# Five and six kept V tiles instead of six and five, and four gradient tiles instead of five, in a decode layer with its gradients

## The chip, the cores and the metric

The kernel runs on one core of one Trainium2 chip. The core has five engines that run on their own and meet at semaphores: TensorE (PE, matrix products and transposes), VectorE (DVE), ScalarE (ACT), GpSimd (POOL) and SyncE (SP, which here only issues DMAs). PEld is the weight load of PE, which overlaps its products. Sixteen DMA engines move data between the main memory (HBM) and the on-chip memory (SBUF); SP, POOL and ACT each feed them through a queue of their own. The metric is the device time of one execution in microseconds, as a median of several.

## The reference

One decode step (one query token for each of B = 2 batches) of a transformer layer, and the gradients of all its inputs but one. With D = 640, H = 32 heads, a cache of 4096 positions and head width 128:

```
h  = x + softmax(q @ k_cache^T * Dh**-0.5) @ v_cache @ wo     q = layernorm(x) @ wq, per batch and head
h2 = h + relu(layernorm(h) @ w1) @ w2
out, vjp = jax.vjp(f, x, k_cache, v_cache, wq, wo, w1, w2)
return (out, *vjp(grad_out))
```

The large arrays are the two caches, 64 tiles (batch, head) of 1 MB each, and their two gradients, of the same size. For one (batch, head) with probabilities p, output gradient go and scaled query qs, the gradient of V is the outer product of p and go, and that of K the outer product of p * (V @ go - dot) and qs. So V is needed twice: once for the output, and again, when the output's gradient is known, for V @ go. The rest is small: the weights (some 5 MB of wq and of wo, 2 MB of w1 and of w2) are read, and their gradients are rank-2 outer products that are written.

## The kernel before, in words

The order of all instructions is written out by hand: Python generators yield after a few instructions each, and the main loop (L1116) decides which generator goes on. The order on an engine is the order in which the loop calls.

**First pass (`p1_iter`, L449), i = 0 to 65.** At step i it loads and transposes K of pair i on PE and computes its scores, turns the scores of pair i-1 into exponentials and multiplies them into K (`pk`, DVE L464), and for pair i-2 multiplies V with that (`m_ps`, PE L457). An iteration has eight parts, k = 0 to 7. The K tile of pair i-1 is given back in part k=5 (L549), the V tile of pair i-2 in part k=7 (L567).

**Second pass (`p2_iter`, L823), one call per turn j = 0 to 64.** A turn reads a V tile again (W in the code), transposes it on PE (`pair_transpose`, `t_ps`), gets V @ go (`dp_ps`), and writes two tiles of 1 MB: gV of turn j and gK of turn j-1. DVE makes each in two halves (`outer_half`, L818, some 1.2 us a half), and POOL stores it (L875 and L856). `turns` (L396) is the order of the pairs in this pass.

**How the passes overlap.** From i = 41 (P2_AT) on, every second iteration of the first pass carries a turn, so that turns 0 to 11 lie in it, turns 12 and 13 in its last two iterations, and turns 14 to 64 behind it. Around both run generators in the background: `middle_gen` (the MLP forward and backward, then `go_group`, which makes go for groups of heads), `fin_gen` (weight gradients, through `ot` tiles that ACT fills and stores) and `gx_gen` (the gradient of x). `fin_gen` and `gx_gen` start when the second batch's w1 work is over.

**Kept tiles.** `KEPT` says how many V tiles at the end of each batch are not given back after the first pass: they stay in SBUF (L564) and the batch's turns begin with them, so they are not loaded again. With (6, 5), 53 of the 64 V tiles are loaded twice. A kept tile holds its place from its load in the first pass to its turn.

**The tiles.** Twelve places of 1 MB in SBUF serve K, V, W, w2 and at first wq (`ld`). `take` takes the place that has been free longest, `give` returns it, and a tile can change its purpose on the way: `share` sets how many places each of the purposes `ld` (loads), `g` (gradient tiles), `f` (`ot` tiles of `fin_gen`) and `q` (wq, w2 and rows of `gx_gen`) is to own, and a place that is given back goes to a purpose that has too few. In the overlap three of the twelve become `g`. Behind the first pass two places are added, and (L1123 and L1133)

```
share(ld=KEPT[1] + 4, g=5)
...
elif fin is not None and j >= H + KEPT[1] - 1:                # L1133
    share(ld=5 + more, g=5 + 2 * more, f=3, q=2 + 3 * more)
```

divides the fourteen: nine for loads, of which five hold kept tiles, and five for gradients. `f` gets one more place (L1145) when `fin_gen` starts. The second `share` holds from turn 36 on. When go is known for all heads, six more places come (L1127: one `ld`, two `g`, three `q`).

**Loads.** `queue` (L1067) lists them in a fixed order: K of i, V of i-2, and W one turn ahead. `pump` issues the next one as soon as `take` has a place, so a load stands in SP's order behind the program step that gave the place back, and on the chip it waits for the last reader of that place. A tile that DVE writes (gK, gV) waits for the DMA that stored the place before.

`go_group` runs over groups of heads: in batch 0 the kept heads first in two groups, (first, first+2) and (first+2, H), then the others by eight; in batch 1 the kept ones in one group, then the others. `MID` (L404) decides which of the heads of batch 0 keep their 128x128 map (L570) in which of two pools.

Of the kernel before, what the change touches and what calls it, by code (L numbers as in the profile page):

```python
# [15 lines left out]
def kernel(  # L16
# [80 lines left out]
    def goes_to(tag):  # L97

        if owned[tag] > wanted.get(tag, len(pools)):
            for other in homes:  # L100
                if owned[other] < wanted.get(other, 0):
                    return other
        return tag
# [14 lines left out]
    def share(**want):  # L118

        wanted.clear()  # L120
        wanted.update(want)
        for tag in homes:
            while free[tag] > 0 and goes_to(tag) != tag:
                to = goes_to(tag)
                homes[to].append(homes[tag].pop(0))
                for d in (free, owned):
                    d[tag] -= 1
                    d[to] += 1

    def more_home(tag, pool):  # L130
        homes[tag].append(len(pools))
        pools.append(pool)
        free[tag] += 1
        owned[tag] += 1
# [257 lines left out]

    pairs = [(b, h) for b in range(B) for h in range(H)]
    NP1 = len(pairs)
    KEPT = (6, 5)
    turns = [(b, h) for b in range(B) for h in (*range(H - KEPT[b], H), *range(H - KEPT[b]))]  # L396
    turn_of = {bh: j for j, bh in enumerate(turns)}
    kept = {(b, h) for b in range(B) for h in range(H - KEPT[b], H)}
    u_bank = [None]
# [3 lines left out]
    MTs = {}  # L403
    MID = H - KEPT[0] - NMT[1]  # L404
    mt_free = [list(range(n)) for n in NMT]
# [313 lines left out]
    def middle_gen(b):  # L719
# [66 lines left out]

        first = H - KEPT[b]
        bounds = [(first, first + 2), (first + 2, H)] if b == 0 else [(first, H)]
# [6 lines left out]
    def ga_gen():  # L795

        gbc = cols.tile([128, Dff], BF16, tag="fbc", name="gbc")
        for b in range(B):
            yield from bcast_cols(one(gc, b), ND, lambda c: 128, gbc[:, b * D:(b + 1) * D])
        for k in range(NW2):  # L800
            while k not in w2_tiles:
                yield 0.0
            t = w2_tiles.pop(k)
            for c in range(k * FP, min(NF, (k + 1) * FP)):
                kc = f_kc(c)
                for b in range(B):
                    yield from turn()
                    ttr(t[0:kc, c - k * FP, :], gbc[0:kc, b * D:(b + 1) * D], ga[0:kc, b, c:c + 1], D, kc)
                    yield 0.9
            give(t)  # L810
# [122 lines left out]
    def fin_gen(fin):  # L933
        FIN["wide"] = [fin.tile([128, 4, 4, 32], BF16, tag="wide", bufs=2, name="wide") for _ in range(2)]
        for w in FIN["wide"]:
            nc.vector.memset(w[:], 0.0)
        yield from wait(2)
        yield from rows_of(fin, acol, NF, "ar", "rX")
        yield from rows_of(fin, gc, ND, "gr", "rD")
        yield from outer_rows(FIN["ar"], Dff, FIN["gr"], D, out_7, Dff // 96)  # L940
        yield from rows_of(fin, ghfc, NF, "ghfr", "rX")
        yield from rows_of(fin, x2c, ND, "x2r", "rD")
        yield from outer_rows(FIN["x2r"], D, FIN["ghfr"], Dff, out_6, ND)
        HH = H // 2
        while ("gh1", B - 1) not in done:
            yield
        yield from rows_of(fin, gh1c, ND, "gh1r", "rD")
        for s0 in range(0, H, HH):
            yield from rows_of(fin, OFc[:, s0:s0 + HH, :], HH, "OFr", "rX")
            yield from outer_rows(FIN["OFr"], HH * 128, FIN["gh1r"], D, out_5[s0 * 128:(s0 + HH) * 128, :], HH)  # L950
        yield from rows_of(fin, x1c, ND, "x1r", "rD")
        for s0 in range(0, H, HH):
            while not all(("go", B - 1, h) in done for h in range(s0, s0 + HH)):
                yield
            yield from rows_of(fin, GQc[:, s0:s0 + HH, :], HH, "GQr", "rX")
            yield from outer_rows(FIN["x1r"], D, FIN["GQr"], HH * 128, out_4[:, s0 * 128:(s0 + HH) * 128], ND)
# [87 lines left out]
    def bg_until(mark):  # L1044
        slot[0] = 99
        forced[0] = True
        while mark not in done:
            assert bg and bg_one(bg) >= 0.0, mark
        forced[0] = False
# [33 lines left out]
    def pump():  # L1083
        while queue:
            what, k = queue[0]
            if what == "w":
                load_weights(k)
            else:
                tag = "ld"
                if free["ld"] < 1:  # L1090
                    return
                if what == "w2":
                    w2_tiles[k] = load_w2(k, tag)
                else:
                    load_tile(what, k, tag)
            queue.pop(0)
# [12 lines left out]
    def p2_step():  # L1109
        nonlocal g2  # L1110
        try:
            next(g2)
        except StopIteration:
            g2 = None

    for n, (i, j) in enumerate(plan):  # L1116
        all_go = all(("go", B - 1, h) in done for h in range(H))
        if i is None and plan[n - 1][0] is not None:
            pkp.release()
            big1 = tc.alloc_tile_pool(name="big1", bufs=1)  # L1120
            for _ in range(2):
                more_home("ld", big1)
            share(ld=KEPT[1] + 4, g=5)  # L1123
        if all_go and not late[0]:
            wop.release()
            big3 = tc.alloc_tile_pool(name="big3", bufs=1, side="right")
            for tag in ("ld", "g", "g", "q", "q", "q"):  # L1127
                more_home(tag, big3)
        late[0] = all_go
        more = int(late[0])  # L1130
        if fin is not None and not bg2 and not bg3:
            share(ld=8 + 3 * more, g=7 + 3 * more)
        elif fin is not None and j >= H + KEPT[1] - 1:  # L1133
            share(ld=5 + more, g=5 + 2 * more, f=3, q=2 + 3 * more)
        if j is not None:
            while g2 is not None:
                p2_step()
            if j < NP1:
                bg_until(("go", *turns[j]))
            g2 = p2_iter(j, 0)  # L1140
        if i is None and ("w1", 1) in done and fin is None:
            wts.release()
            fin = tc.alloc_tile_pool(name="fin", bufs=1)
            big2 = tc.alloc_tile_pool(name="big2", bufs=1)
            more_home("f", big2)  # L1145
            banks.update(sps=[2, 3], o=[4, 5, 6])
            bg2.append(("fin", fin_gen(fin)))
            bg3.append(("gx", gx_gen(fin)))
        if i == 12:
            bg.append(("ga", ga_gen()))  # L1150
        if i == H + 2:
            banks["bc"].insert(0, banks["sps"].pop(0))
        elif i == P2_AT:
            banks["bc"].remove(7)
            banks["sps"].insert(0, banks["bc"][0])
            banks["bc"] = [7]
        rate = RATES[0 if i is not None and i <= H + 1 else 1 if j is None and i < P2_AT else
                     2 if i is not None else 3 if j <= H else 4]
        if i is None:
            spread[0] = 2  # L1160
            at_k[0] = 1
            k = 0
            while g2 is not None:
                p2_step()
                pump()
                slot[0] = int(k in ((1, 3, 5) if j <= H else (1, 4)))
                k += 1
                bg_step(0, rate)
                bg_step(1, RATE2)
                bg_step(2, RATE3)  # L1170
            continue
        at = MIXED if j is not None else REST
        for k, _ in enumerate(p1_iter(i, i < H + 1, 0)):
            for _ in range(at.get(k, 0)):
                if g2 is not None:
                    p2_step()
            if k == 5:
                a_heads(i)
            pump()

            spread[0] = 1 if i < P2_AT else 2
            at_k[0] = k
            if i >= P2_AT:
                slot[0] = int(k == 6 or (k == 1 and j is None))
            elif i > H + 1:
                slot[0] = {1: 2, 3: 1, 4: 1, 6: 1}.get(k, 0)
            else:
                slot[0] = int(k in (1, 6))
            bg_step(0, rate)
            bg_step(1, 0.0)  # L1190
        if i is not None and i in (H + 1, NP1 + 1):
            bg.append((f"m{i // H - 1}", middle_gen(i // H - 1)))
# [41 lines left out]
```

## Time and profile before

| | |
|---|---|
| median of 3 runs | 908.89 us (908.7 to 909.97) |
| span of the profiled execution, first to last instruction | 905.5 us |
| its mean granted TensorE clock | 0.780 |
| busy PE, PEld | 742.8 us (82%), 620.3 us (68%) |
| busy DVE, ACT, POOL | 696.1 us (77%), 444.7 us (49%), 192.4 us (21%) |
| DMA | 362.87 MB, mean 401 GB/s |
| Vt, Kt loads, issue to landing (median) | 15.9 us, 16.0 us |
| Wt loads | 11.8 us |
| gV, gK stores | 14.7 us, 14.4 us |

No separate time is recorded for the profiled execution; what is known of it is its span, which lies 3.4 us below the median of the timed runs.

How to read it: an engine's share is an average over the whole span. The profile gives busy times and DMA rates for any stretch of it too, and the kernel has several stages: the first pass alone (to about 266 us), the overlap (to about 463 us), and the second pass alone. The DMA row counts how long its sixteen engines had packets, GB/s what they moved: both matter, for a queue with little in it can look busy and move less. Where an engine waits, the profile names the instruction or the DMA that ended the wait.

### The profile page before, as it was taken

The numbers are of one execution on the slowest core, as the hardware profiler recorded it, in microseconds if no ns is written. First come the engines' busy times: TensorE is split into PE (matmuls) and PEld (weight loads), VectorE is DVE, ScalarE is ACT, GpSimd is POOL, SyncE is SP. The second block draws the span as 40 slices with busy tenths as digits, with TensorE's granted clock in tenths as the row PEclk, the third lists the DMA queues.
The fourth block names the chain that finished last, engine by engine and source line by source line (L and its number), as shares of the span: only waits on it lengthen the run. The fifth ranks groups of instructions, "written<-read, shape, count | busy, mean of one in ns | idle before, by whom it ended". The sixth has DMA issues, their size and how long they took to land.

```text
span 905.5 us, 24516 instructions
## 1 busy us (share of the span) xinstructions
PE 742.8 (82%) x10205; PEld 620.3 (68%) x10205; DVE 696.1 (77%) x1286; ACT 444.7 (49%) x1096; POOL 192.4 (21%) x330
## 2 busy tenths in 40 slices
PE   3999899899998997987968854877899879859880
PEld 3887788788887887876857744655667656645560
DVE  2666787777888796777869698986898349989982
ACT  1444343344554564554543434644576656637750
POOL 1344433443211110010011111211122111111120
PEclk9999999999999899999885776655555555555655
DMA  8999999999879999999999999999999999999997
GB/s 361 420 409 403 409 398 410 420 417 388 335 306 377 377 406 425 421 424 421 411 398 392 411 423 394 423 398 396 407 401 388 426 420 423 419 423 416 419 421 296
DMA packets 56254, 362.87 MB, mean 401 GB/s; under 512 B 5680, under 2 KB 11696, under 8 KB 15312
## 3 DMA queue, kind: packets, MB, share of 16 engines
q1 hardware_dynamic: 34704, 212.18, 58.1%
q0 software_dynamic: 18432, 134.23, 35.9%
q10 hardware_dynamic: 3008, 14.91, 4.2%
q8 instruction: 80, 1.31, 0.6%
q14 instruction: 30, 0.25, 0.1%
HBM read 212.16 MB, written 149.13 MB: 399 GB/s over the span
## 4 chain that ended last, share of the span: by engine, by line
PE 42%; DMA 25%; DVE 18%; issue 6%; ACT 6%; SPq 1%; POOL 0%; POOLq 0%; ACTq 0%; DVEq 0%
PE t_ps L423 18%; DMA Vt<-in_A_v_cache_dram 13%; PE m_ps L457 9%; DVE gV L818 5%; DMA out_dram<-gV 4%; DVE gK L818 4%; DMA out_dram<-gK 3%; PE s_ps L436 3%; ACT t_sb L428 3%; DMA wqs<-in_A_wq_dram 3%; DVE gxj L644 2%; PE u_ps L486 2%; PE o_ps L922 2%; PE dp_ps L436 2%; DVE pk L464 2%
## 5 line engine op out<-in xcount | busy, mean ns | idle before, releaser
L428 ACT COPY t_sb<-t_ps 128x512 f32<-128x512 f32 x479 | 274.4, 586 | 214.6 <-PE t_ps L423 208.9
L436 PEld LDWEIGHTS <-t_sb 128*128 128x128 bf16 x4096 | 179.0, 102 | 47.0 <-issue 18.8
L423 PE MATMUL t_ps<-ident_f,Wt 128*128 128x128 f32 x848 | 196.5, 379 | 0.2 <-ACT t_sb L428 0.2
L457 PE MATMUL m_ps<-pk,Vt 128*128 128x129 bf16 x2048 | 171.0, 222 | 19.5 <-DMA Vt<-in_A_v_cache_dram 18.2
L464 DVE TENSOR_TENSOR pk<-Kt,ep 128x2048 bf16<-128x2048 bf16 x128 | 156.5, 1223 | 33.9 <-PE m_ps L457 15.8
L818 DVE TENSOR_TENSOR gK<-rb,gsp 128x2048 bf16<-128x2048 bf16 x128 | 152.4, 1225 | 18.4 <-DMA out_dram<-gV 16.4
L818 DVE TENSOR_TENSOR gV<-rb,pp 128x2048 bf16<-128x2048 bf16 x128 | 153.0, 1219 | 15.1 <-DMA out_dram<-gK 12.5
L423 PE MATMUL t_ps<-ident_f,Kt 128*128 128x128 f32 x1024 | 155.1, 284 | 6.6 <-DMA Kt<-in_A_k_cache_dram 6.3
L423 PEld LDWEIGHTS t_ps<-ident_f,Wt 128*128 128x128 f32 x848 | 135.7, 196 | 35.1 <-issue 29.3
L457 PEld LDWEIGHTS <-Vt 128*128 128x128 bf16 x2048 | 124.5, 98 | 51.0 <-issue 29.7
L423 PEld LDWEIGHTS t_ps<-ident_f,Kt 128*128 128x128 f32 x1024 | 112.6, 144 | 10.9 <-PE s_ps L436 4.6
L474 POOL COPY pk<-ep 128x16 bf16<-128x16 bf16 x80 | 83.2, 1042 | 163.6 <-ACT ep L512 87.8
L436 PE MATMUL dp_ps<-gom,t_sb 128*128 128x2 bf16 x2048 | 95.6, 168 | 8.5 <-ACT t_sb L428 7.5
L875 POOL DMA_DIRECT2D out_dram<-gV x64 | 34.2, 534 | 268.0 <-DVE gV L818 207.7
L856 POOL DMA_DIRECT2D out_dram<-gK x64 | 34.0, 532 | 264.9 <-DVE gK L818 207.8
L436 PE MATMUL s_ps<-qm,t_sb 128*128 128x2 bf16 x2048 | 87.4, 164 | 1.5 <-DVE t_sb L426 1.5
L928 ACT CAST ot<-o_ps 128x512 bf16<-128x512 f32 (+4 forms) x160 | 70.4, 490 | 14.8 <-DMA out_dram<-ot 11.2
L571 ACT CAST MT<-m_ps 128x128 bf16<-128x128 f32 x64 | 17.1, 267 | 104.3 <-PE m_ps L457 104.2
L845 ACT ACTIVATE rb<-dp_ps,rt 128x256 bf16<-128x256 f32 x64 | 30.3, 474 | 69.4 <-PE dp_ps L840 68.7
L644 DVE CUSTOM_DVE_ANT_0 junk<-wo_t,hbc 128x640 bf16<-128x640 bf16 x64 | 52.4, 819 | 0.2
L644 DVE CUSTOM_DVE_ANT_0 gxj<-wqs,gqr 128x1024 bf16<-128x1024 bf16 x40 | 48.8, 1221 | 2.4 <-DMA wqs<-in_A_wq_dram 2.2
L831 DVE SCALAR_TENSOR_TENSOR gsp<-dp_ps,negdot,P_bf 128x64 bf16<-128x64 f32 x64 | 18.0, 281 | 42.3 <-PE dp_ps L436 42.0
(198 smaller groups left out, 719.5 us busy)
## 6 DMA issues: line engine op xcount, KB each, us to landing
Kt<-in_A_k_cache_dram SPq DMA_DIRECT2D x64, 1024.0 KB, 16.0
Vt<-in_A_v_cache_dram SPq DMA_DIRECT2D x64, 1024.0 KB, 15.9
out_dram<-gV POOLq DMA_DIRECT2D x64, 1024.0 KB, 14.7
out_dram<-gK POOLq DMA_DIRECT2D x64, 1024.0 KB, 14.4
Wt<-in_A_v_cache_dram SPq DMA_DIRECT2D x53, 1024.0 KB, 11.8
wq_t<-in_A_wq_dram SPq DMA_DIRECT2D x5, 1024.0 KB, 9.2
wo_t<-in_A_wo_dram SPq DMA_DIRECT2D x4, 1280.0 KB, 19.1
wqs<-in_A_wq_dram SPq DMA_DIRECT2D x5, 1024.0 KB, 17.1
```

The costliest lines, as they stand in the source:

```text
L423: nc.tensor.transpose(t_ps[:, j, :], natf[:, 2 * cc:2 * cc + 2, :].rearrange("p c k -> p (c k)"), ident_f[:])
L428: nc.scalar.copy(out=t_sb[:], in_=t_ps[:])
L436: nc.tensor.matmul(dst[:, sc:sc + 2], lhsT=v[:, j, :, par], rhs=vecs[:, par, :], start=(par == 0), stop=(par == 1))
L457: nc.tensor.matmul(r["m"][:, 0:129], lhsT=r["V"][:, sc, :], rhs=r["pk"][sc // HALF][:, sc % HALF, 0:129], start=(sc == 0), stop=(sc == NSC ...
L464: nc.vector.tensor_tensor(out=p["pk"][k][:, :, 0:128].rearrange("p s (a two) -> p s a two", two=2), in0=p["K"][:, sl, :].rearrange("p s (a ...
L474: nc.gpsimd.tensor_copy(out=col, in_=e)
L644: nc.vector.tensor_tensor_reduce(out=junk[0:kc, 0:width], in0=in0, in1=in1, scale=1.0, scalar=0.0, op0=ALU.mult, op1=ALU.add, accum_out=acc)
L818: nc.vector.tensor_tensor(out=pairs_view(dst[:, sl, :]), in0=row.rearrange("p (a two) -> p a two", two=2)[:, None, :, :].to_broadcast([128 ...
L845: nc.scalar.activation(out=rb[:], in_=bank[:, 128:384], func=ACT.Copy, scale=rt[:, b, h:h + 1])
L856: nc.gpsimd.dma_start(out=natural(out_2, bp, hp), in_=gK[:])
L875: nc.gpsimd.dma_start(out=natural(out_3, b, h), in_=gV[:])
L928: nc.scalar.copy(out=ot[0:P, k, n0:n0 + nn], in_=o_ps[0:P, 0:nn])
```

## The change

```
-    KEPT = (6, 5)
+    KEPT = (5, 6)
...
             big1 = tc.alloc_tile_pool(name="big1", bufs=1)
             for _ in range(2):
                 more_home("ld", big1)
-            share(ld=KEPT[1] + 4, g=5)
+            share(ld=KEPT[1] + 4, g=4)
```

The first batch keeps five V tiles and the second six. `KEPT` is used in four more places: the order of the turns (L396), the set of kept pairs (L398), `MID` (L404), and the bounds of the groups in `middle_gen` (L787). So turn 5 is now a head whose V is loaded again, and turn 37 (head 31 of batch 1) one whose V was kept; the second `share` holds from turn 37 instead of 36. With `KEPT[1]` = 6, the first `share` gives loads ten places, of which six hold kept tiles, and gradients four, so that the sum stays fourteen. The number of tiles loaded twice stays 53.

## The prediction

> **What bounds the kernel now.** I read the page first (span, DMA and its GB/s, HBM bytes), then busy time and DMA rate by stretch, then the chain of waits with PE's and SP's timelines at two places where loads come late, and last what VectorE (DVE) waits for in the stage with the changed `g`.
>
> ```profile
> span 905.5 us, 24516 instructions
> DMA  8999999999879999999999999999999999999997
> GB/s 361 420 409 403 409 398 410 420 417 388 335 306 377 377 406 425 421 424 421 411 398 392 411 423 394 423 398 396 407 401 388 426 420 423 419 423 416 419 421 296
> HBM read 212.16 MB, written 149.13 MB: 399 GB/s over the span
> ```
>
> The transfers set the time. The slices top out near 424 GB/s; 362.87 MB at that rate would take 856 us, so 905.5 holds about 50 us in which DMA was not full. The change moves no byte in total, so its price is only how much of those 50 us it fills or adds. Where are they? By stretch (last two columns: DMA's busy share, GB/s):
>
> ```profile
> 200.00:310.00 110.00, 103.33 (x1758) 90.70 (x1755) 88.24 (x216) 56.89 (x157) 24.16 (x39) 0.97 0.92 357
> 310.00:450.00 140.00, 123.56 (x1987) 108.49 (x1987) 108.33 (x217) 74.36 (x206) 14.17 (x24) 0.94 1.01 418
> 450.00:460.00 10.00, 9.29 (x165) 7.78 (x163) 8.79 (x18) 5.06 (x14) 2.02 (x3) 1.00 0.95 351
> 480.00:530.00 50.00, 43.73 (x586) 39.49 (x586) 41.65 (x76) 25.49 (x47) 9.28 (x21) 0.65 1.00 403
> 560.00:660.00 100.00, 79.66 (x741) 64.41 (x741) 84.38 (x145) 54.81 (x125) 18.37 (x37) 0.57 1.01 404
> 660.00:700.00 40.00, 37.78 (x338) 28.38 (x337) 36.22 (x68) 28.98 (x67) 10.15 (x18) 0.54 0.98 392
> 700.00:890.00 190.00, 150.98 (x1332) 110.55 (x1331) 153.85 (x208) 111.42 (x235) 30.37 (x63) 0.55 1.01 420
> ```
>
> From 200 to 310 PE is busy 94% and DMA moves 357 GB/s: compute sets the pace and loads wait for tiles. From 310 to 450 DMA is full. From 480 to 700 it is nearly full (392 to 404), and from 700 on full again (420).
>
> **Part A, one V tile fewer kept in batch 0.** Following `take` and `give` through the plan, from i=33 to turn 5 (i=51) one more of the 12 tiles carries loads, and every K and V load moves one place ahead. V of i=43, now issued at i=43 k=7, goes out at k=6. That load is the one place before 310 us where PE stands still for data:
>
> ```profile
> 282.08 9.89 DMA Vt<-in_A_v_cache_dram
> 292.02 0.64 PE L457 MATMUL m_ps<-pk,Vt 128*128 128x129 bf16 x8 [2.36 <-DMA Vt<-in_A_v_cache_dram]
> ```
>
> PE waits 2.36 us, and the windows then show its granted clock at 0.57 for 8 us (292 to 300). SP's V loads around it stand at 288.96 and 300.94, 12.0 us apart, where the neighbours are 7.3: 4.7 us lost. With the change K45 goes out at about 273.4 instead of 280.38 and V43 at 280.4, before the queue fills, and the stall should be gone. Behind 310 us transfers set the pace, so what counts is bytes moved earlier. One tile more ahead is 1.049 MB / 424 GB/s = 2.5 us. The dip after the stall, 300 to 307 at 318 GB/s, lost 7 x (1 - 318/424) = 1.75 us, of which I take half, since compute bounds part of it. Sum -3.3 us, bounds -4.7 (the whole late iteration) and 0 (the lead is used up before 310).
>
> The reload that this costs (turn 5's V, 1 MB) enters at i=47 and leaves the last stage: 29 W loads in a row become 28. Both places are full of transfers (418 and 404 to 420), so 2.5 us move and the sum is 0. Its issue on SP takes 0.33 us; SP only waits for tiles there, so nothing stands behind it but later loads that have no tile yet. Group (0..8) of batch 0 is due at turn 5 instead of 6. It is recorded in turn 4's iteration, two iterations ahead of need, so nothing is forced: 0. If that cover were gone, its eight products of 0.82 us (L644) would stand in front of the turn: 6.6 us. Groups of 2+3 instead of 2+4 heads, 6 instead of 5, and the map tiles of L570 are the same work in another place: 0.
>
> **Part B, one V tile more kept in batch 1.** From V of i=58 on one tile fewer carries loads, until turn 37 has used the last kept one. V61 cannot go out with K63:
>
> ```profile
> 425.31 1.57 SPq L444 DMA_DIRECT2D Vt<-in_A_v_cache_dram  x1
> 437.99 0.33 SPq L444 DMA_DIRECT2D Wt<-in_A_v_cache_dram  x1
> 439.18 0.33 SPq L444 DMA_DIRECT2D Vt<-in_A_v_cache_dram  x1
> ```
>
> The first of these rows is V61. It must now wait for K60's tile, which today goes to the W load at 437.99, and each later load slips a place. SP issues nothing between 427 and 438, and the queued megabytes keep DMA at 410 to 426. With one less it runs out 2.5 us earlier, and 450 to 460 (351 GB/s) has no spare work to fill it: +2.5 us. Behind SP's waiting instruction stand the W loads of turns 12 to 14. W of turn 14 would go out at about 462.3 instead of 455.0 and is due at 468.8; V of i=43 above took 9.9 us to land, so PE may stand about 3 us. PE is idle from 470 to 478 anyway, waiting for DVE, which covers it; without that cover 3 us more. Bounds 0 and +5.5.
>
> **Part C, four gradient tiles instead of five, turns 14 to 36 (463 to about 656 us).** What DVE waits for in this stretch, and two stores from the chain with their time to landing:
>
> ```profile
> DVE gK L818 <- DMA out_dram<-gV: 15.0, 8, 4.0
> DVE gV L818 <- DMA out_dram<-gK: 8.5, 7, 2.3
> 584.02 18.62 DMA out_dram<-gK
> 612.40 21.59 DMA out_dram<-gV
> ```
>
> DVE waits 15 times, 23.5 us, for a store to free a tile. With four, a half tile may start when the store four back has landed, not five back. Setting each start between 455 and 645 against the landing of the store four back gives 68 us of overlap in place of 23.5, were landings unchanged. They are not: a full queue lands its stores sooner when fewer stand in it. In 535 to 550 PE does nothing, no loads go out, and stores alone keep DMA at 423 to 429, so there a late DVE costs nothing. What costs is the emptier queue in the dips. The nearest rows: 700 to 890 has six more tiles (one `ld`, two `g`, three `q`) and 420 GB/s, 560 to 660 has 404. That is 2.7 GB/s for a tile, over some 195 us 2.7/404 x 195 = 1.3 us. A tile taken from few is worth more than one added to many, so I take +2.0. Lower bound -1 (fewer stores ahead of each W load). Upper bound: the stretch's loss today, 195 x (1 - 404/424) = 9 us, doubles.
>
> The Trainium skill bears on this part twice. Its page "DMA: Bandwidth & Descriptors", section "Anatomy of one DMA — SWDGE (gpsimd) path", gives a store as about 2.0 us plus bytes over 436 GB/s; an estimate from it is 4.4 us for this megabyte, and by it three stores in flight would suffice and part C would be 0. The trace's first store, alone in its queue, does land in 4.3 us; under load the rows above show 18.6 and 21.6, so I do not use it. Its page "Perfetto Trace Analysis", section "Optimization Strategy", says that the same gap repeating on the engine that should be saturated can mean too few buffers for the next tile; the 15 waits of DVE are such gaps, and by that rule the change goes the wrong way here, by a price it does not state.
>
> **Part D, the output tiles.** `share` at L1134 now waits for turn 37, so `f` gets its second and third tile one turn later. In the built order the 18 `ot` tiles fall behind, and the last is taken at turn 62 instead of 60. Stores of `ot` go out at 664.5, 672.9 and 677.5 now, in a stretch at 392 GB/s; one of them moves out of it into a full stretch. Half a megabyte to one is 1.2 to 2.5 us: I take +1.3, bounds 0 and +5 (two move). At the end two turns of 5.5 us (gV stores at 875.71, 881.47, 886.80) put the last `ot` at about 882, before the last gK store at 889.39, which lands 14.4 later; that covers it.
>
> **Sum.** -3.3 + 2.5 + 2.0 + 1.3 = +2.5 us. On the profiled execution's span: 905.5 to 908.0. The median of the runs, 908.89, lies 3.4 above that span, and I leave this difference as it is: **911.4 us**. The forecast's own range is 910.7 to 914.5.
>
> **The rivals.**
> The lead holds (faster): part A gives its full 4.7, B is hidden because DMA has queued stores at 440 to 460, and C and D are near 0.5 together, as stores alone keep DMA at 425. For it: the stall and the 12.0 us iteration are plain in the trace, and full stretches don't care for one tile. Against: the tile that is given at 33 is taken back at i=58, some 220 us later. 908.9 - 4.7 + 0.5 = 904.7.
> The starved ring (slower, more): DVE, 96% busy from 760 to 860 and 84% from 560 to 660, becomes the bound in turns 14 to 36, because each fifth tile was what let it work ahead while W loads took the queue. Its price is up to part C's 9 us, from the point where DVE's waits pass about 45 us; with B and D and less A: 908.9 + 9 + 3.8 - 3.3 = 918.4. Against: DMA is full there with stores alone.
> A swap (no change): A and B are the same tile at two places and cancel, C and D are hidden by the full queue: 908.9.
>
> **How the numbers follow.** Two runs of this kernel can't be told apart within about 0.2%, 1.8 us. Forecast (+1.8 to +6) 0.40, starved ring (over +6) 0.15, lead holds 0.28, swap 0.17. So faster 0.28, same 0.17, slower 0.55. The range reaches beyond the faster rival's centre to 903.5 and close to the starved ring's, 918, which leaves out about 0.2.
>
> **What would show it.** A: no PE wait of over 2 us on V between 280 and 300, no half clock there, and the gV store of turn 2 (305.35 now) some 4 us earlier. B: a gap in DMA between 425 and 460, V61 issued near 438 less A's gain, 450 to 460 under 351 GB/s. C: DVE waits for stores over 35 us between 455 and 660, with the rate there under 402; if waits grow and the rate stays, C is 0. D: `ot` stores later by one to two turns, and 660 to 700 under 392. I am wrong if the end of the first loop does not move up by about 3 us, or if the last stage, from the first turn without i to the end, does not lengthen.

## The result, and the profile after

The changed kernel takes 913.62 us, the median of 22 runs (908.84 to 919.13); 22 runs of the kernel before beside it have a median of 909.31 us (905.15 to 914.26). The ratio is 1.0042, 95% interval 1.0024 to 1.0060: 3.8 us slower (2.2 to 5.5). A second set of runs gave 1.0042 again (1.0011 to 1.0073). The forecast was 2.5 us slower, 911.4 us, with a range of 903.5 to 918; the result lies in it, on the side that had most of the chance.

Single executions of one kernel differ by about 1% here (35 runs of the kernel before: 904.59 to 915.94), so two profiles differ by some us in places where the programs are the same. Below, a reading counts as shown only where it returns in several kernels with the same part, or in the times; what rests on one profile or one run is called so.

The page of the changed kernel:

```profile
span 909.3 us, 24519 instructions
DMA  8999999999889999999899999999999999999997
GB/s 363 419 410 404 409 399 410 421 417 400 340 306 367 422 423 422 422 421 423 356 387 423 389 424 386 395 394 411 378 399 384 399 371 425 425 424 427 423 424 320
HBM read 212.16 MB, written 149.13 MB: 397 GB/s over the span
```

No byte was added, and the mean rate fell from 399 to 397 GB/s. The dips have moved: 356 and 387 in the 20th and 21st slice (432 to 477 us), 378 and 384 between 636 and 705, 371 at 727 to 750.

Busy time by stretch of the changed kernel, in the columns of before (PE, PEld, DVE, ACT, POOL, granted clock, DMA's busy share, GB/s):

```profile
200.00:310.00 110.00, 105.16 (x1829) 92.57 (x1828) 91.68 (x217) 61.03 (x169) 24.28 (x40) 1.00 0.93 365
310.00:450.00 140.00, 121.14 (x1944) 106.49 (x1942) 105.84 (x218) 72.60 (x200) 14.71 (x24) 0.93 1.00 415
450.00:460.00 10.00, 9.59 (x181) 8.29 (x180) 8.63 (x17) 4.88 (x14) 1.88 (x3) 1.00 0.91 341
480.00:530.00 50.00, 42.58 (x556) 38.46 (x556) 39.66 (x71) 24.47 (x45) 7.90 (x19) 0.62 1.00 407
560.00:660.00 100.00, 70.91 (x696) 57.15 (x695) 80.40 (x138) 50.67 (x117) 16.86 (x36) 0.60 0.99 390
660.00:700.00 40.00, 37.08 (x331) 28.17 (x331) 36.83 (x62) 26.27 (x57) 9.11 (x18) 0.54 0.98 394
700.00:890.00 190.00, 152.89 (x1335) 112.37 (x1335) 151.77 (x215) 115.92 (x249) 29.14 (x63) 0.54 1.00 412
```

Against before, the rate is up from 357 to 365 in the first row, down from 404 to 390 at 560 to 660, and down from 420 to 412 behind 700. (The first row alone is no proof: lead, with the same part A, has 349.)

The place of part A, first in the kernel before and then in the changed one:

```profile
292.00:300.00 8.00, 7.61 (x87) 6.57 (x88) 4.18 (x6) 3.23 (x8) 0.53 (x1) 0.57 1.01 425
```

```profile
292.00:300.00 8.00, 7.66 (x123) 6.68 (x123) 6.50 (x9) 5.06 (x14) 0.53 (x1) 1.00 1.01 425
```

PE is equally busy in both, and issues 87 products in the one and 123 in the other: at half the clock each takes longer. In the changed kernel no wait on V is left among PE's waits from 280 to 300 us, and the half clock is gone there. A stall like it comes later, in the changed kernel at 338.82:

```profile
338.82 0.64 PE L457 MATMUL m_ps<-pk,Vt 128*128 128x129 bf16 x8 [2.53 <-DMA Vt<-in_A_v_cache_dram]
```

All seven profiles with five tiles kept first have such a wait there (1.3 to 2.5 us at 337 to 342 us), and PE's waits on K and V from 275 to 430 us sum to 14.4 and 12.6 us in the two profiles of the changed kernel, 13.6 before. So part A puts a stall off, and does not take it away.

The place of part B, SP's loads of the changed kernel (start, duration, and the idle time before where there is one; "x4" puts four together):

```profile
423.27 0.33 SPq L444 DMA_DIRECT2D Kt<-in_A_k_cache_dram  x1
437.99 0.33 SPq L444 DMA_DIRECT2D Vt<-in_A_v_cache_dram  x1
439.18 0.33 SPq L444 DMA_DIRECT2D Wt<-in_A_v_cache_dram  x1
445.29 0.33 SPq L444 DMA_DIRECT2D Vt<-in_A_v_cache_dram  x1
452.72 0.33 SPq L444 DMA_DIRECT2D Wt<-in_A_v_cache_dram  x1
454.42 0.33 SPq L444 DMA_DIRECT2D Vt<-in_A_v_cache_dram  x1
462.44 5.96 SPq L444 DMA_DIRECT2D Wt<-in_A_v_cache_dram  x4
```

V61 goes out at 437.99 instead of 425.31, and W of turn 14 at 462.44 instead of 455.03: both as priced. In the six profiles with six tiles kept last V61 goes out at 436.4 to 438.0, in the eight others at 422.9 to 431.6. DMA runs thin over it: 360 GB/s from 430 to 440 and 383 from 440 to 450, where the kernel before has 419 in both (after_again: 404 and 389). PE's waits on it, first before and then in the changed kernel:

```profile
477.36 0.67 PE L594 MATMUL a_ps<-OFc,wo_t 128*128 128x1 bf16 x20 [7.95 <-DVE OFc L585]
```

```profile
471.82 1.09 PE L423 MATMUL t_ps<-ident_f,Wt 128*128 128x128 f32 x4 [3.37 <-DMA Wt<-in_A_v_cache_dram]
477.23 0.67 PE L594 MATMUL a_ps<-OFc,wo_t 128*128 128x1 bf16 x20 [4.33 <-DVE OFc L585]
```

PE stands 3.37 us for the late W, and so much less for DVE after it: the product of L594 starts at the same time.

The place of part C, what DVE waits for from 455 to 660 us in the changed kernel (total us, times, longest):

```profile
DVE gK L818 <- DMA out_dram<-gK: 12.7, 8, 4.2
DVE gV L818 <- DMA out_dram<-gV: 8.9, 8, 2.4
DVE gK L818 <- DMA out_dram<-gV: 4.9, 2, 4.4
...
DVE gV L818 <- DMA out_dram<-gK: 1.6, 2, 0.9
```

With five tiles gK waited for a gV store and gV for a gK store, five stores back; with four each mostly waits for its own kind, four back. The waits are 28.1 us instead of 23.5, hardly more, because the stores land sooner. The pages' lines of the stores, with the median time from issue to landing at the end, before and then changed:

```profile
out_dram<-gV POOLq DMA_DIRECT2D x64, 1024.0 KB, 14.7
out_dram<-gK POOLq DMA_DIRECT2D x64, 1024.0 KB, 14.4
```

```profile
out_dram<-gV POOLq DMA_DIRECT2D x64, 1024.0 KB, 10.9
out_dram<-gK POOLq DMA_DIRECT2D x64, 1024.0 KB, 10.6
```

A store that lands sooner is here no gain in time. That it stood behind fewer others, so that less was queued for DMA when the loads paused, is the likely reading; it is argued, not shown.

### The profile page after: what moved, and what is told of

Its sections match the earlier page's. It is cut to its first block, busy times and chain, and to the rows that moved or that the text cites. A ratio compares the mean times of both kernels' runs of the same rounds, so it can differ in the third digit from the quotient of the medians.

```text
span 909.3 us, 24519 instructions
## 1 busy us (share of the span) xinstructions
PE 743.9 (82%) x10205; PEld 622.6 (68%) x10205; DVE 696.4 (77%) x1286; ACT 445.9 (49%) x1096; POOL 190.3 (21%) x330
## 4 chain that ended last, share of the span: by engine, by line
PE 42%; DMA 24%; DVE 20%; issue 7%; ACT 5%; SPq 1%; POOL 0%; ACTq 0%; POOLq 0%; DVEq 0%
PE t_ps L423 18%; DMA Vt<-in_A_v_cache_dram 13%; PE m_ps L457 9%; DMA out_dram<-gK 6%; DVE gV L818 5%; DVE gK L818 4%; DMA out_dram<-gV 4%; DVE gxj L644 4%; PE s_ps L436 3%; PE o_ps L922 3%; PE u_ps L486 2%; ACT t_sb L428 2%; DVE pk L464 2%; DVE junk L644 2%; PE dp_ps L436 2%
## 5 line engine op out<-in xcount | busy, mean ns | idle before, releaser
L423 PE MATMUL t_ps<-ident_f,Kt 128*128 128x128 f32 x1024 | 158.4, 288 | 6.3 <-DMA Kt<-in_A_k_cache_dram 6.3
L818 DVE TENSOR_TENSOR gV<-rb,pp 128x2048 bf16<-128x2048 bf16 x128 | 153.0, 1219 | 10.6 <-DMA out_dram<-gV 8.9
L423 PEld LDWEIGHTS t_ps<-ident_f,Kt 128*128 128x128 f32 x1024 | 114.7, 146 | 10.6 <-issue 4.9
## 6 DMA issues: line engine op xcount, KB each, us to landing
out_dram<-gV POOLq DMA_DIRECT2D x64, 1024.0 KB, 10.9
out_dram<-gK POOLq DMA_DIRECT2D x64, 1024.0 KB, 10.6
```

Of the source, the lines that this page charges most:

```text
L423: nc.tensor.transpose(t_ps[:, j, :], natf[:, 2 * cc:2 * cc + 2, :].rearrange("p c k -> p (c k)"), ident_f[:])
L818: nc.vector.tensor_tensor(out=pairs_view(dst[:, sl, :]), in0=row.rearrange("p (a two) -> p a two", two=2)[:, None, :, :].to_broadcast([128 ...
```

## The experiments

All are timed against the kernel before on the same chip; a ratio has its 95% interval, and us are the ratio less one, times 909. "Turn" of the second share is where `elif fin is not None and j >= H + KEPT[1] - 1` (L1133) first holds, in the kernel before 36, in the changed one 37.

**lead.** Part A alone, with one more V tile loaded again.

```
-    KEPT = (6, 5)
+    KEPT = (5, 5)
```

> KEPT = (5, 5) with five gradient tiles and the shares of before: part A alone, and one V tile more is read again (1.05 MB, 2.5 us at 424 GB/s). By the record -3.3 + 2.5 = -0.8 us, ratio 0.999, and the gV store of turn 2 comes 4 to 5 us earlier after the store of turn 0 than before. If the lead is worth nothing in a run that transfers bound: +2.5 us, 1.0028. If the lead keeps its whole 4.7 us: -2.2 us, 0.9976.

Measured: 909.07 us, ratio 0.9999 [0.9977, 1.0020], -0.1 us (-2.1 to +1.8). What is measured is that part A and the added load cancel. Less 2.5 us for that load (1.049 MB at 424 GB/s, an estimate: no run times a load alone) part A is worth -2.6 us. PE has no wait on V at 280 to 300 in this kernel either.

**ring4s35.** Part C alone: four gradient tiles with six and five kept ones; the place goes to W, and the second share is moved so that `ot` tiles are taken in the same turns as before.

```
-            share(ld=KEPT[1] + 4, g=5)
+            share(ld=10, g=4)
...
-        elif fin is not None and j >= H + KEPT[1] - 1:
+        elif fin is not None and j >= H + 3:
```

> The kernel before with four gradient tiles and ten load tiles in the first share (KEPT stays at 6, 5), and the second share from turn 35, so that the ot tiles are taken in the turns of before. Part C alone: W loads get the tile that the stores lose. By the record +2.0 us, ratio 1.0022, nothing different up to 460 us, DVE waits for stores over 35 us between 455 and 660. The starved ring says +9 us, 1.010. If four tiles are as good as five: 1.000, with the last stage as long as before.

Measured: 911.37 us, ratio 1.0016 [0.9991, 1.0040], +1.5 us (-0.8 to +3.6). It agrees with part C's +2.0, and does not exclude 0.

**share35.** The change without part D, as it was meant.

```
-    KEPT = (6, 5)
+    KEPT = (5, 6)
...
-            share(ld=KEPT[1] + 4, g=5)
+            share(ld=KEPT[1] + 4, g=4)
...
-        elif fin is not None and j >= H + KEPT[1] - 1:
+        elif fin is not None and j >= H + 3:
```

> The changed kernel, but the second share holds from turn 35, so that the 18 ot tiles are taken in the same turns as before the change (the last in turn 60). It has parts A, B and C and not D. By the sum on record D is 1.3 us: ratio to the kernel before about 1.0028 (+2.5 of the measured +3.8). If the late output tiles are the main cause (the trace after has its last three turns 8 us apart, with the last ot stores at 878, 887 and 893): ratio 1.000 or below, and the last three turns 5 to 6 us apart again. If the ring of gradient tiles is the main cause: 1.004, with the same lag of 5 to 9 us at turn 31 as after the change.

Measured: 916.70 us, 6 runs, ratio 1.0072 [1.0045, 1.0098], +6.5 us. The sum of the recorded A, B and C is +1.2, so this is a miss. It is also 2.7 us above the whole change, uncertain by some 3; taken at face value it would give part D a price of -2.7.

**lag.** Parts B and C, one tile less to load again, and the `ot` tiles one turn later.

```
-    KEPT = (6, 5)
+    KEPT = (6, 6)
...
-            share(ld=KEPT[1] + 4, g=5)
+            share(ld=10, g=4)
...
-        elif fin is not None and j >= H + KEPT[1] - 1:
+        elif fin is not None and j >= H + 4:
```

> KEPT = (6, 6), ten load and four gradient tiles, the second share from turn 36: parts B and C and a little of D without A, and one V tile less is read again (-2.5 us). By the record +2.5 + 2.0 + 0.6 - 2.5 = +2.6 us, ratio 1.003, with V of pair 61 issued some 13 us later than before. If what batch 1 keeps costs nothing at the end of the first loop: about 0, 1.000. If the last stage alone makes the loss: the lag against before at turn 13 is under 1 us and grows only after it.

Measured: 915.34 us, ratio 1.0057 [1.0030, 1.0083], +5.2 us. The recorded B and C less 2.5 for the load give +2.0 and at most +1.3 more for D. This too is more than the sum, and I first took it for a larger part B: with six kept tiles only eight places work from turn 14 to 36. Of the next four runs, eight35 and ring5_35 test that, the other two part D.

**eight35.** The kernel before with eight working places: nine for loads, of which five hold kept tiles, four gradient tiles, and one place put aside.

```
-            share(ld=KEPT[1] + 4, g=5)
+            share(ld=KEPT[1] + 4, g=4, q=1)
...
-        elif fin is not None and j >= H + KEPT[1] - 1:
+        elif fin is not None and j >= H + 3:
```

> The kernel before (six and five kept tiles) with the first share at nine places for loads, four for gradients and one for rows that do not come yet, so that one of the fourteen places stands idle until turn 35, and with the second share at turn 35 so that the output tiles are taken in the same turns as before. Up to the end of the first loop nothing differs. W has four places and gradients four, as in the changed kernel: eight working places where the kernel before has nine and ring4s35 (which moves the place to W) nine. The recorded steps know only the queue of gradients: C's +2.0 us, 910.9 to 911.7, the same as ring4s35, which measured +1.5. The theory formed since, that part B's price lies in the last stage (a sixth kept tile of batch 1 takes a place out of the ring from turn 14 to 36) and not in the one transition that was priced, expects +4 to +6 us, a ratio of 1.005 to 1.006, with the gV stores of turns 14 to 34 some 8 us later than before.

Measured: 912.60 us, ratio 1.0032 [1.0005, 1.0058], +2.9 us (+0.5 to +5.3). Its middle lies under the +4 to +6 of that theory and its interval reaches into it; it is not far from ring4s35, which has the ninth place at work.

**ring5_35.** The changed kernel's kept tiles, with five gradient tiles and three places for W.

```
-    KEPT = (6, 5)
+    KEPT = (5, 6)
...
-            share(ld=KEPT[1] + 4, g=5)
+            share(ld=9, g=5)
...
-        elif fin is not None and j >= H + KEPT[1] - 1:
+        elif fin is not None and j >= H + 3:
```

> The changed kernel with nine places for loads and five for gradients in place of ten and four: of the nine, six hold kept tiles, so W has three places. The second share is put at turn 35, as in share35, so that this kernel and share35 (+6.5 us) differ in nothing but which purpose has the eighth working place. If the cost is the number of working places, this one is at share35's time or some us from it, 914 to 918. If the cost is the shorter queue of gradient tiles itself (part C as recorded), it is faster than share35 by 2 us or more. If W loads with three places come late, PE waits for them and it is slower than share35, over 918.

Measured: 908.84 us, ratio 0.9997 [0.9969, 1.0025], -0.3 us. The interval is -2.8 to +2.3 us. Also eight working places, and no loss: the theory of a larger B falls. This is A and B together in the changed kernel's own kept tiles, at -0.3 (recorded: -0.8). With A at -2.6, which rests on the estimate for a load, B is +2.3, the recorded +2.5.

**late38.** Part D alone: the kernel before, with the `ot` tiles taken in the turns of the changed kernel.

```
-        elif fin is not None and j >= H + KEPT[1] - 1:
+        elif fin is not None and j >= H + 6:
```

> The kernel before with the second share two turns later (from turn 38 in place of 36), so that the output tiles are taken in the turns in which the changed kernel takes them, the last at turn 62. Nothing else differs: part D alone. The recorded term expects +1.3 us (0 to +5), about 910.4 to 911. The difference between the changed kernel and share35, which differ in little but this (-2.7 us, each ratio uncertain by 2 us), expects -2 to -3 us, some 906.5 to 907.5. A null of 0 would say that the output tiles' turns do not matter and that the -2.7 was scatter.

Measured: 912.16 us, ratio 1.0032 [1.0001, 1.0064], +2.9 us (+0.1 to +5.8). D costs here, as recorded, with an interval that barely leaves out 0; for the kernel before the reading of -2.7 falls. The stretch from 690 to 890 us, in the kernel before, then in late38:

```profile
690.00:890.00 200.00, 160.69 (x1416) 117.41 (x1416) 161.82 (x226) 118.39 (x251) 32.93 (x68) 0.56 1.01 420
```

```profile
690.00:890.00 200.00, 162.41 (x1427) 120.66 (x1427) 158.29 (x226) 122.42 (x264) 30.75 (x66) 0.54 1.00 412
```

PE and ACT have nearly the same work (1 and 3% more), and DMA moves 8 GB/s less. From 690 to 720 alone it is 387 instead of 422, and from 720 on 417 instead of 420.

**leadlate38.** lead with the same late `ot` tiles, as a kernel that might beat both.

```
-    KEPT = (6, 5)
+    KEPT = (5, 5)
...
-        elif fin is not None and j >= H + KEPT[1] - 1:
+        elif fin is not None and j >= H + 6:
```

> Five kept tiles in both batches, five gradient tiles, the second share from turn 38: the kernel lead with the output tiles of the changed kernel. It loads one V tile more than either (1 MB, 2.5 us at 424 GB/s). Part A by lead is then -0.1 - 2.5 = -2.6 us, and this kernel tells whether late output tiles are worth something beside it. The recorded D expects lead + 1.3, a ratio of about 1.001; the reading of share35 against the changed kernel expects lead - 2.7, a ratio of about 0.997, which would beat both kernels.

Measured: 912.26 us, ratio 1.0024 [0.9997, 1.0050], +2.2 us, and so 2.3 above lead, uncertain by some 3: the same sign once more.

**share35_again and after_again.** The same two kernels side by side, to see whether share35 was scatter.

> share35 once more (five and six kept tiles, four gradient tiles, the second share at turn 35), beside the changed kernel itself in the same call. The term D as late38 and as leadlate38 against lead measured it (+2.9 and +2.3 us) expects this kernel about 2.5 us under the changed one, a ratio of some 1.002 to 1.003: then the 6.5 us of share35 were scatter. If share35's loss is its own, because dividing the places at turn 35 while three of six kept tiles are still held starves the ring (its profile moved 306 to 320 GB/s from 660 to 680 us, the changed kernel 379 to 418), it is again at +5 to +7 us and again under 350 GB/s there, and then it is no measure of the change without D.

> The changed kernel as it is, in the same call as share35_again, eight38 and six_g4, so that differences between them do not hang on the chip or the hour. Expected 1.004 as before, +2 to +5.5 us. Additive terms (A -2.6, B +2.3, C +1.5, D +2.5) expect +3.7.

Measured: share35_again 1.0073 [1.0046, 1.0100], after_again 1.0042 [1.0011, 1.0073]. Both times share35 lies clear above the sum of +1.2 (lower ends +4.1 and +4.2), so that is not scatter. Above the changed kernel it is by 2.7 and 2.8 us, uncertain by 3 to 4 each time, so the order of the two is likely, and not shown. Where the traces differ: the stretch from 660 to 690 in share35_again, then in after_again:

```profile
660.00:690.00 30.00, 27.69 (x228) 19.72 (x228) 25.90 (x42) 20.63 (x46) 6.62 (x12) 0.50 0.85 348
```

```profile
660.00:690.00 30.00, 26.38 (x267) 20.05 (x266) 28.95 (x45) 19.62 (x42) 7.20 (x13) 0.67 0.98 396
```

And SP's W loads between 641 and 704 us, first those of share35, then of the changed kernel (first and last start at the end of the line; the load before the first stands at 639.9 and 639.8):

```profile
L444 SPq DMA_DIRECT2D Wt<-in_A_v_cache_dram x2: 327/328/328, 692.7 to 699.5; - x2
```

```profile
L444 SPq DMA_DIRECT2D Wt<-in_A_v_cache_dram x2: 328/328/328, 655.1 to 662.2; - x2
```

The second `share` lowers `ld` to five. While kept tiles still count among the places of `ld`, that means no W load until turn 40. At turn 35 with six kept tiles the pause begins two loads early: 52.8 us without a load from 639.9, where the kernel before has 38 (645.3 to 683.4), and DMA runs at 0.85 of its time. So share35 is not simply the change without D: it adds a dip of its own, and the later second share of the changed kernel, turn 37, is what keeps its loads going to 662. lag, at turn 36 with a tile kept for turn 37, has the same dip (342). But that the early pause makes the whole loss is not shown: ring5_35 has its second share at turn 35 too, pauses a load earlier still (633.4 to 679.0), and loses nothing.

**eight38.** Parts C and D together, without A and B: eight35 with `j >= H + 6` in the second edit.

> eight35 (the kernel before with eight working places, four of them for gradients, and one idle) with the second share at turn 38: parts C and D together, without A and without B's transition. If D adds to C as it added to the kernel before (late38, +2.9), it is at +5 to +6 us, a ratio of 1.006. If late output tiles cost nothing or help where there are only four gradient tiles (the changed kernel against share35 by their first runs, -2.7), it is at 0 to +3 us.

Measured: 918.52 us, 8 runs, ratio 1.0109 [1.0070, 1.0148], +9.9 us. C and D do not help each other; together they cost more than their sum: eight35 and late38 give +5.8, and against eight35 D costs +7.0 here. W loads pause to 709.9, the latest of all (362 GB/s at 690 to 720, 414 behind), but where all of the other 4 us are isn't settled.

**six_g4.** The dose the other way: six gradient tiles and three places for W.

```
-            share(ld=KEPT[1] + 4, g=5)
+            share(ld=KEPT[1] + 3, g=6)
...
-        elif fin is not None and j >= H + KEPT[1] - 1:
+        elif fin is not None and j >= H + 4:
```

(The second line is the same turn as before.)

> The kernel before with eight places for loads and six for gradients in place of nine and five: three places for W (as in ring5_35, where that cost nothing) and one gradient tile more. Output tiles in the same turns as before. The dose the other way: if what counts in turns 14 to 36 is the queue of gradient tiles, as part C has it, the kernel gains what a tile is worth at the other end, by the recorded slope of 2.7 GB/s for a tile -1.3 us, by the loss of four tiles -1.5 to -3, a ratio of 0.997 to 0.9985, faster than both kernels. If five tiles are enough for a full queue, 0. If three W places are too few without the sixth kept tile, slower by 1 us or more.

Measured: 910.83 us, ratio 1.0005 [0.9981, 1.0029], +0.5 us. DVE's waits for stores between 455 and 660 fall from 23.5 to 16.7 us, and nothing is gained: those waits are not what the time goes by. The run takes a place from W at the same time, so it does not show that a sixth tile by itself is worth nothing.

None of these kernels beats both. lead and ring5_35 are level with the kernel before, and it stays the best together with them.

**All of them by stretch.** GB/s in the stretch of each part, from one profile of each kernel; W is the number of places that work for W loads, "share" the turn of the second share, "resume" the time at which W loads go on after their pause behind 630 us.

| kernel | kept | g | W | share | ratio | 430 to 470 | 560 to 660 | 660 to 690 | 690 to 890 | 690 to 720 | resume |
|---|---|---|---|---|---|---|---|---|---|---|---|
| before | 6, 5 | 5 | 4 | 36 | 1 | 401 | 404 | 384 | 420 | 422 | 683.4 |
| changed | 5, 6 | 4 | 4 | 37 | 1.0042 | 364 | 390 | 395 | 411 | 386 | 704.5 |
| after_again | 5, 6 | 4 | 4 | 37 | 1.0042 | 382 | 390 | 396 | 414 | 383 | 703.5 |
| share35 | 5, 6 | 4 | 4 | 35 | 1.0072 | 377 | 389 | 330 | 419 | 393 | 692.7 |
| share35_again | 5, 6 | 4 | 4 | 35 | 1.0073 | 371 | 390 | 348 | 419 | 394 | 691.2 |
| ring5_35 | 5, 6 | 5 | 3 | 35 | 0.9997 | 372 | 390 | 369 | 421 | 415 | 679.0 |
| lag | 6, 6 | 4 | 4 | 36 | 1.0057 | 371 | 396 | 342 | 412 | 369 | 704.9 |
| ring4s35 | 6, 5 | 4 | 5 | 35 | 1.0016 | 419 | 396 | 384 | 420 | 397 | 690.2 |
| eight35 | 6, 5 | 4 | 4 | 35 | 1.0032 | 378 | 393 | 368 | 423 | 425 | 680.9 |
| eight38 | 6, 5 | 4 | 4 | 38 | 1.0109 | 410 | 392 | 399 | 406 | 362 | 709.9 |
| late38 | 6, 5 | 5 | 4 | 38 | 1.0032 | 409 | 402 | 397 | 412 | 387 | 698.0 |
| lead | 5, 5 | 5 | 4 | 36 | 0.9999 | 391 | 401 | 398 | 419 | 400 | 687.9 |
| leadlate38 | 5, 5 | 5 | 4 | 38 | 1.0024 | 384 | 393 | 407 | 412 | 373 | 707.2 |
| six_g4 | 6, 5 | 6 | 3 | 36 | 1.0005 | 385 | 394 | 396 | 420 | 417 | 678.8 |

One cell alone tells little; groups do. From 430 to 470 the six kernels with six kept tiles in the second batch have 373 in the mean, the eight with five have 397. From 690 to 890 the five with a share at 37 or 38 have 411, the eight others but lag 420; lag, whose loads resume as late as theirs, has 412. From 560 to 660 the eight with four gradient tiles have 392, the five with five 398, six_g4 with six 394. This last split hangs on the kept tiles too: with five and six kept, the four profiles with four gradient tiles have 389 to 390, and ring5_35 with five has 390, which loses no time.

## Why the prediction was right

By the windows and by the times its terms come out so:

| part | recorded | from the traces' groups | from the times |
|---|---|---|---|
| A | -3.3 (-4.7 to 0) | -3.5 | -2.6 (lead) |
| B | +2.5 (0 to +5.5) | 40 x (397 - 373)/424 = +2.3 | +2.3 (ring5_35 less A) |
| C | +2.0 (-1 to +9) | 100 x (398 - 392)/424 = +1.4 | +1.5 (ring4s35), +2.9 (eight35) |
| D | +1.3 (0 to +5) | 200 x (420 - 411)/424 = +4.2, less what 660 to 690 gains: +3.4 | +2.9 (late38), +2.3 (leadlate38), +7.0 (eight38 less eight35) |
| sum | +2.5 | +3.6 | +3.5 to +5.5 without eight38, measured +3.8 (2.2 to 5.5) |

(+3.4 is 230 x (415.7 - 409.4)/424, from 660 to 890, where the five late kernels are set against the six others without share35 and lag.) Each figure from the times is uncertain by 2 to 4 us either way, so that C could be nothing by ring4s35 alone, and A and B each rest on one run and on the estimate of 2.5 us for a load.

What is measured in the changed kernel's own kept tiles are two sums. A + B is -0.3 (ring5_35, with three W places and its share at 35; recorded -0.8), and C + D, the step from ring5_35 to the changed kernel, is +4.1, uncertain by some 3 (recorded +3.3). So the forecast was right in that the move of a kept tile is nearly free, to some 2.5 us either way, and that the ring and the share cost the time. How C + D divides is not shown. In kernels with five tiles kept last C is +1.5 to +2.9 and D +2.3 to +7.0; by way of share35 C would be +6.8 and D -2.7. Nor do the parts simply add: share35, lag and eight38 lie 2 to 5 us above their sums, where the whole change is 3.8. That the recorded sum of four came within 1.3 us of the measured one is in part luck.

**A, its sign came where it was named; its price is not shown.** The first figure in its third column is the move of gV stores between turn 0 and turn 4 against the kernel before, which leaves out where a run starts: -3.1 to -4.7 in the seven profiles with five tiles kept first, -1.8 to +0.7 in the seven with six; -4.1 less -0.6. PE waits on V between 275 and 305 us in all seven of the latter (0.7 to 2.6 us, 1.6 in the mean) and in none of the former. The store of turn 2 was to be some 4 us earlier than 305.35; it stands at 302.17. But the stall returns near 338 us, as shown above, and the lead can't be followed to the end of the loop: against turn 0, gV of turn 12 is 1.6 us earlier than before in the five profiles with five and six kept, 0.3 later in the two with five and five, and 1.2 earlier in the six with six and five; the reload and part B lie between. The step on V43 came out otherwise too: it goes out at 282.64, not at 280.4; what moved is K45, to 275.36. That the reload costs 0 where it moves, no run tests by itself.

**B, right in place; its size fits.** V61 near 438, W of turn 14 at 462.3 (462.44 measured), 450 to 460 under 351 GB/s (341): all came. The wait of PE on the late W, priced at about 3 us and as covered by its wait for DVE, came too: 3.37 and 3.45 us in the two profiles, with 4.33 and 4.31 left of 7.95 for DVE. after_again has 356 in the 10 us from 450, so the rate there alone is no proof; the group over 40 us is a better one, though eight35, the kernel before up to 463 us, has 378 in it.

**C, possible in size; its sign was half wrong.** DVE was to wait over 35 us for stores, and waits 28.1. The step that sized this, "68 us of overlap ... were landings unchanged", was bounded in the same breath by sooner landings, and they took more of it than I left in the sign. The other half came: the rate from 455 to 660 is 398 GB/s (405 before), under the 402. It singles out little, for lead and ring5_35 with five tiles have 401 and lose nothing. That a missing tile costs by an emptier queue and not by a waiting DVE fits this, and eight35 (DVE waits 23.7 us, as before, and +2.9 us), but it is not shown. The two rules weighed there: by the Trainium skill's page "DMA: Bandwidth & Descriptors", the estimate of 4.4 us for a store made C 0; stores took 10.6 to 10.9 us in the median with four tiles, and eight35 excludes 0, barely (+0.5), with a second share one turn earlier beside it. By "Perfetto Trace Analysis" repeated gaps can mean too few buffers; four were likely too few, while six_g4 took away nearly a third of the gaps and gained nothing, so the gaps by themselves did not price a tile.

**D, right in sign where it could be run alone, too small, and at another place.** The step "one of them moves out of it into a full stretch" expected 660 to 700 to fall under 392 GB/s. It has 394. What the later share takes from the `ot` stores there it gives to W loads, which go on to 662 us. The loss lies behind 690, over half of it from 690 to 720, where the rate falls from 422 to 386. The `ot` stores don't account for a lower rate (one is issued in these 30 us before, two after). The W loads do: in all fourteen profiles the rate there goes with the time at which they resume, 415 to 425 GB/s where that is by 684 us, 362 to 387 where it is 698 or later. The prediction followed the places that this share gives to `f` and left out that the same share stops the loads. How much of D is this pause and how much the `ot` stores, no run separates. With five tiles kept last D is 2.3 to 2.9 us in place of 1.3, and 7.0 with four gradient tiles as well. The cover at the end held, though the last turns are 8 us apart instead of 5.5: the last `ot` store is issued at 893.09 instead of about 882, 8 us before the last gK store (901.18), and that one lands in 6.4 us instead of 14.4, so that 11.8 us of later issue become 3.8 at the end.

**The conditions for being wrong** were drawn badly in one place. The end of the first loop was to move up by 3 us, but B's price falls due at 430 to 460, inside that loop: by the prediction's own terms it should move by -3.3 + 2.5 = -0.8. (It also moved the reload's 2.5 us into this loop and out of the last stage; but up to 465 us both kernels have issued 11 W loads, so the loop took in no load more. The turns behind the second batch's kept tiles have 27 and 26 W loads, where it counts 29 and 28; and its own range ends at 914.5 where +6 would give 914.9. Nothing else rests on these.) Against turn 0, gV of turn 12 stands 1.4 and 1.7 us earlier in the two profiles. From that store to the landing of the last gK store it takes 442.6 and 442.9 us instead of 438.9, +3.7 and +4.0, where C and D were +3.3. Both fit, but neither is sharp: the six kernels with six and five kept, the same program up to turn 14, have gV of turn 12 anywhere from 3.0 us earlier to 0.8 later than before.

**The rivals.** The lead holds: A + B measured -0.3, not -4.7, and DMA fell to 360 GB/s at 430 to 440, so B was not hidden. The starved ring: DVE's waits never came near 45 us. A swap: A and B do nearly cancel (-0.3 by the times), but C and D together are not hidden.

**What stays open.** In the kernels with six tiles kept last, share35 and ring5_35 differ in one place given to W or to gradients, and by 6.8 us, uncertain by some 3.5. That is more than C's 1.5 to 2.9 in the kernels with five. Part of it lies in the longer pause (52.7 and 51.3 us against 45.6, with 330 and 348 against 369 GB/s at 660 to 690, about 2 us), the rest isn't explained. So in the changed kernel itself the sign of D alone stays open. The changed kernel with five gradient tiles, three W places and its own share at 37, which would part C from D there, wasn't run.

## What to carry over

The waits of the engine that fills a buffer did not price it here: VectorE's waits for stores were 16.7 us with six tiles (six_g4, +0.5 us), 23.5 with five, and 23.7 and 27.9 with four (eight35, +2.9, and ring4s35, +1.5). Where transfers set the time, look instead for the stretches in which one kind of transfer pauses: the GB/s from 690 to 720 went with the end of the W loads' pause in every kernel. A stall that is gone from its place may have moved on; sum the waits over the whole stage before pricing it. And a constant that sets several things at once (here the kept tiles, the date of a share and the order of turns) can't be undone in one place alone: the run that was to undo part D added a dip of its own, and the same part in three other kernels cost 2.3, 2.9 and 7.0 us.

## What was not expected of the hardware

Landing times rose with the number of stores that the program lets into the queue, but not by that alone. A gV store alone in the queue landed in 4.3 us (before). The medians of gV stores were 10.9 to 12.8 us in the eight profiles with four tiles, 12.8 to 15.1 in the five with five, and 14.8 with six.

Waits of PE of some 2.5 us for a load were followed by a lower granted clock. The one of 2.36 us was followed by 8 us at 0.57, with PE 95% busy in them; one of 2.56 us in eight38 by 0.59 in the same 8 us, one of 2.50 in six_g4 by 0.50 from 297 to 300. Without the stall the same stretch runs at 1.00, and so it does after the waits of 0.75 to 0.99 us in lag, ring4s35 and eight35.
